# Undivided agent values in the product, a GpSimd fold of the sums, and a linear product issued in steps: agent attention with a maxout layer

## The chip, the cores and the metric

The kernel runs on one core of a Trainium2 chip. The metric is the device time of one execution in microseconds (us). Six runs of the kernel before gave a median of 465.62 us, from 465.35 to 466.1. The profile comes from one execution, so times inside it are compared with that execution's own time. PE is TensorE, PEld its weight loads, DVE is VectorE, ACT is ScalarE, POOL is GpSimd, and SP is SyncE, which issues the transfers.

## The reference, cut to what matters

```
a2k     = softmax(scale * agents @ k^T)      # per batch: 49 agents over 12544 keys
agent_v = a2k @ v                            # 49 x 128
q2a     = softmax(scale * q @ agents^T)      # 12544 queries over 49 agents
x       = q2a @ agent_v                      # 4 batches: 50176 rows of 128
h       = max(x @ w1, x @ w2, x @ w3)        # 768 wide
out     = h @ w_out
```

There are 4 batches. The softmax of the agents over the keys divides each agent's row of `agent_v` by one number, the sum of that agent's exponentials.

## The kernel before, in words

**What is computed.** The maxout is rewritten with differences: max(x w1, x w2, x w3) = x w1 + max(0, x (w2 - w1), x (w3 - w1)) (one of the six slices uses w3 - w2 in place of w3 - w1). So each batch needs a small matrix G: agent_v times the weights' differences (columns C31 and C21, 768 each) and agent_v times w1 w_out (256 columns from C1O, the linear part, for two row halves). A query group then needs only its exponentials `e_q`, G and `w_out`. The 128 partitions are split in two halves (h) of 64, each with the 49 agents, for even and odd rows.

**Key groups.** Keys are worked in groups of up to nine 128-row tiles (`k_group`): load k and v (SP), cast to bf16 (POOL for k; ACT or POOL for v), transpose k, scores (L291, PE), exponentials (L296, ACT), values (L302, PE), and an addition into `Vacc` (L312, DVE). The first batch's twelve groups run before any query ("early"). They transpose on PE (L273) and copy the result on DVE (L279), and they sum the exponentials with a matmul against ones (L305, 49 columns, giving every partition the sum of each agent, in `Vacc`'s columns 49 to 97). The later three batches' groups are hosted one by one in query groups, share their small PSUM tile, and add their exponentials on POOL into `Eacc` (L319). Two of these transpose on PE, the rest by a DMA issued from SP (L275).

**The tail of a batch's keys** (`k_tail`). `reduce` sums `Eacc` over its nine positions on DVE (L363, 441 to 49 columns). `total` sums it over the partitions with a float32 matmul against ones (L368). `normalise` takes the reciprocal (L374), clears 15 columns (L376) and multiplies `Vacc` by it into `avT` (L377). `product` multiplies `avT` by pieces of the weights (L389), and DVE (L394) or ACT (L396) copies the result into G.

**Query groups** (`q_group`, 49 of them, s = 0 to 48, each 8 tiles): cast, transpose (L454 and the copy L459, or a DMA), scores (L474), exponentials (L480), their sums (L488) and reciprocals (L494). Then for six slices f: `first` (u, L500), `relu_first` (a, L515, or L512 in place for one slice), `second` (v, L500) and `max_second` (x, L525 on DVE, or L523 on ACT). Then the output: `out_linear` (L530, needs G's linear part), `out_hidden` (L539) and `out_scale` (L546), and the store (L553).

**The order.** Every step is put on a list with a key by `at`, and `emit` issues them sorted by key, one program order for all engines; a query group spans 6.0 keys, and the tables KEY, LATE, BORDER and BEGIN give each step's place in it. A step whose needs are not met, or whose ring of buffers is not free, is held back until they are. The rings are "uv" (3 PSUM tiles of two banks for u, v and products), "om" (2 small PSUM tiles, for query transposes, scores, the hosted key work and outputs) and "a". Each engine then runs its own instructions in this order and waits on semaphores.

**Borders and the ramp.** Query groups 12, 24 and 36 are the first that need the next batch's G; the group before each runs the tail of its keys (the "border"). The "ramp" is the change from the early groups to the steady order, groups 0 and 1. There `ramp` issues six filler matmuls (L624) of 512 columns in place of the output matmuls of a group that does not exist. `prep_linear1` computes w1 w_out (six matmuls, L227, and a copy on ACT, L228), and the third piece of G's product follows it. `keep_busy` (L233) issues other fillers.

Of the kernel before, what the change touches and what calls it, by code (L numbers as in the profile page):

```python
# [9 lines left out]
FP32 = mybir.dt.float32  # L10
BF16 = mybir.dt.bfloat16
# [5 lines left out]
def kernel(  # L17
# [18 lines left out]
    nc = tc.nc  # L36
# [130 lines left out]
    agT = const.tile([P, B, H], BF16, name="agT")  # L167
    nc.vector.memset(agT, 0.0)
    sel = const.tile([P, 2], BF16, name="sel")
    nc.vector.memset(sel, 0.0)  # L170
# [52 lines left out]

    def prep_linear1():
        t = small_tile("o_ps")
        for f in range(NF):
            nc.tensor.matmul(t[:, :C], w1T[:, f, :], wo_bf[:, f, :], start=(f == 0), stop=(f == NF - 1))  # L227
        nc.scalar.activation(wall[:, C1O + C:C1O + 2 * C], t[:, :C], AF.Copy)  # L228

# [13 lines left out]
    def k_group(b, t0, n, key, s):  # L243
# [38 lines left out]
        def scores():  # L282
            if early:
                d["pair"] = uv_tile()
                d["s"] = d["pair"][:, 0, :]
                last_tile["t"] = d["s"]
            else:
                d["s"] = host[s]
            t = d["s"]
            for j in range(n):  # L290
                nc.tensor.matmul(t[:, j * A:(j + 1) * A], d["kT"][:, j, :], agT[:, b, :A],  # L291
                                 start=(j == 0), stop=True, skip_group_check=True)

        def exps():
            d["e"] = work.tile([P, KT * A], BF16, tag="e_k", bufs=3, name="e_k")
            nc.scalar.activation(d["e"][:, :n * A], d["s"][:, :n * A], AF.Exp, scale=scale)  # L296

        def values():
            t, c = (d["pair"][:, 1, :], 0) if early else (d["s"], CV)
            for j in range(n):  # L300
                e = d["e"][:, j * A:(j + 1) * A]
                nc.tensor.matmul(t[:, c:c + A], d["vb"][:, j, :], e, start=(early and j == 0),  # L302
                                 stop=True, skip_group_check=True)
                if early:
                    nc.tensor.matmul(t[:, A:2 * A], ones_bf, e, start=False, stop=True,  # L305
                                     skip_group_check=True)

        def add_values():
            w = 2 * A if early else A
            src = d["pair"][:, 1, :w] if early else d["s"][:, CV:CV + A]  # L310
            if t0:
                nc.vector.tensor_tensor(out=Vacc[b], in0=src, in1=Vacc[b], op=ALU.add)  # L312
            else:
                Vacc[b] = work.tile([P, w], FP32, tag=f"Vacc{w}", name="Vacc")
                nc.vector.tensor_copy(out=Vacc[b], in_=src)
# [42 lines left out]
    def k_tail(b, sum_key, keys, s):  # L358
        d = {}

        def reduce():
            d["e"] = work.tile([P, A], FP32, tag="e_sum", name="e_sum")
            nc.vector.tensor_reduce(out=d["e"], in_=Eacc[b].rearrange("p (j a) -> p a j", a=A),  # L363
                                    axis=mybir.AxisListType.X, op=ALU.add)

        def total():
            d["s"] = host[s]
            nc.tensor.matmul(host[s][:, :A], ones, d["e"], start=True, stop=True,  # L368
                             skip_group_check=True)

        def normalise():

            r = (last_tile["t"] if s is None else d["s"])[:, :A]
            nc.vector.reciprocal(r, Vacc[b][:, A:] if s is None else r)  # L374
            d["avT"] = work.tile([P, H], BF16, tag="avT", name="avT")
            nc.vector.memset(d["avT"][:, A:], 0.0)  # L376
            nc.vector.tensor_tensor(out=d["avT"][:, :A], in0=Vacc[b][:, :A], in1=r, op=ALU.mult)  # L377
            G[b] = work.tile([P, WC], BF16, tag="G", name="G")

        def product(c0, c1, on_vector):  # L380
            t = uv_tile()
            cuts = [c for c in range(c0, c1, 512)] + [c1]
            for i, (a, z) in enumerate(zip(cuts, cuts[1:])):
                for lo, hi in ((a, min(z, C1O)), (max(a, C1O), z)):
                    for h in range(2 if lo < hi else 0):


                        c = lo + (C if lo >= C1O and h == 0 else 0)
                        nc.tensor.matmul(t[h * H:(h + 1) * H, i, lo - a:hi - a], d["avT"],  # L389
                                         wall[:, c:c + hi - lo], start=True, stop=True,  # L390
                                         skip_group_check=True)
            src = t.rearrange("p i c -> p (i c)")[:, :c1 - c0]
            if on_vector:
                nc.vector.tensor_copy(out=G[b][:, c0:c1], in_=src)  # L394
            else:
                nc.scalar.activation(G[b][:, c0:c1], src, AF.Copy)  # L396

        if s is not None:
            at(sum_key - 1, reduce, ("sum_e", b), [("kx", s - 1)])
            at(sum_key, total, ("total", s), [("sum_e", b), ("ho", s)])  # L400
        at(sum_key + (0.9 if s is None else 0.01), normalise, ("normalise", b),
           [("ka", ("early", NT - last_size)) if s is None else ("total", s)])

        pieces = ((C31, C1O), (C21, C31), (C1O, WC)) if s is None else ((C31, WC), (C21, C31))
        for i, (c0, c1) in enumerate(pieces):
            on_vector = s is None and i == 0
            at(keys[i], lambda c0=c0, c1=c1, on_vector=on_vector: product(c0, c1, on_vector),
               ("product", b, i), [("normalise", b)] + ["lin_b"] * (i == 2), "uv", [("product", b, i)])

# [12 lines left out]
    def q_group(s):  # L422
# [132 lines left out]
        new = [("product", tails[s], i) for i in range(2)] if s in tails else []  # L555
        new_linear = new if s else [("product", 0, 2)]

# [54 lines left out]
    def ramp():  # L612

        for o in range(1, 2):
            at(KEY[f"lin{o}"] - 6, lambda: d_fill.update(t=small_tile("o_ps")), ("fill", o), (), "om",
               [("filled", o)])
            keys = sorted(KEY[f"oc{o}{f}"] for f in range(NF))
            for i, key in enumerate(keys):
                at(key - 6, fill, ("filled", o) if i == NF - 1 else None, [("fill", o)])

    d_fill = {}

    def fill():
        nc.tensor.matmul(d_fill["t"], ident, busy, start=True, stop=True, skip_group_check=True)  # L624

# [4 lines left out]
    first_key = last_key - 6.0 * (len(first_sizes) - 1)  # L630
    last_size = first_sizes[-1]
    at(first_key - 35, prep, "prep", (), "om", ["prep"])
    at(first_key - 6.5, load_weights)
# [3 lines left out]
    at(last_key - 3.24, prep_w_out)  # L637
    at(4.5, prep_linear1, "lin_b", ["lin_a"], "om", ["lin_b"])
    fillers = []
    for g, n in enumerate(first_sizes):  # L640
        k_group(0, sum(first_sizes[:g]), n, first_key + 6.0 * g, None)

        if 4 <= g < len(first_sizes) - 5:
            fillers += [(first_key + 6.0 * g + 0.55, 3), (first_key + 6.0 * g + 1.3, 3)]
    k_tail(0, last_key, (last_key + 0.95, last_key + 1.02, 4.8), None)
    for key, n in fillers + [(last_key + 0.9, 2), (last_key + 1.1, 2),
# [47 lines left out]
```

## Time and profile before

| what | value |
|---|---|
| median of six runs | 465.62 us |
| the profiled execution: its time / its span | 466.1 us / 464.3 us |
| granted TensorE clock | 1.000 |
| PE busy | 437.1 us (94%), 5450 matmuls |
| DVE busy | 405.7 us (87%) |
| ACT busy | 396.4 us (85%) |
| POOL busy | 167.1 us (36%) |
| L525, maximum on DVE | 245 of 1220 ns |
| L539, output matmuls on PE | 2352 |
| L363, reduction on DVE | 3 of 946 ns |
| L319, additions on POOL (441 columns) | 27 of 1026 ns |

Busy time of an engine is a share of the whole span, and the stages have different limits, so the stages are read apart. A matmul's length in the rows is about 0.2 to 0.4 us with its way through the array, and the next starts long before it ends: what matmuls cost is read from start to start. In the time line, a bracket after a row gives the idle time before it and what ended it.

### The profile page before, as it was taken

The page shows a single profiled execution, that of the slowest core. Times are in us where ns is not written, and L with a number is a line of the kernel's source. Part 1 is how long each engine was busy: PE and PEld are TensorE (multiplying, and loading weights), DVE is VectorE, ACT ScalarE, POOL GpSimd, SP SyncE. Part 2 cuts the span into 40 slices and gives each one's busy share as a digit, 9 for nine tenths or more (in the row PEclk, how much of TensorE's full clock was granted, in tenths as well). Part 3 has the DMA queues.
Part 4 walks back from the last instruction along what each step waited for, and adds up shares of the span by engine and source line. Part 5 has one row for each costly group of instructions (what it writes and reads, how often), then busy time and mean ns, then how long its engine had stood idle before and what let it go on. Part 6 is the DMA issues. An engine that isn't in the chain of part 4 may idle for free.

```text
span 464.3 us, 13292 instructions
## 1 busy us (share of the span) xinstructions
PE 437.1 (94%) x5450; PEld 274.7 (59%) x5450; DVE 405.7 (87%) x516; ACT 396.4 (85%) x461; POOL 167.1 (36%) x167
## 2 busy tenths in 40 slices
PE   2497899999999999999999999999999999999996
PEld 2375466666665766666656666666656555555554
DVE  3165699999998999999999999999998999999995
ACT  3356889989899999899889898998999999999992
POOL 2244963553450544536262446354230010100000
PEclk9999999999999999999999999999999999999999
DMA  8999999999998999998997999996846668553222
GB/s 317 409 410 392 409 284 380 292 350 213 310 288 285 288 287 324 317 271 221 293 335 246 288 315 306 293 257 182 186 114 180 162 172 171 163 134 114 69 85 98
DMA packets 82632, 118.53 MB, mean 255 GB/s; under 512 B 56391, under 2 KB 57867, under 8 KB 82571
## 3 DMA queue, kind: packets, MB, share of 16 engines
q1 hardware_dynamic: 82368, 117.59, 84.3%
q8 instruction: 42, 0.69, 0.6%
q14 instruction: 19, 0.16, 0.1%
q10 hardware_dynamic: 203, 0.10, 0.1%
HBM read 78.74 MB, written 25.69 MB: 225 GB/s over the span
## 4 chain that ended last, share of the span: by engine, by line
PE 82%; DMA 6%; ACT 6%; issue 2%; DVE 2%; POOL 0%; SPq 0%; ACTq 0%; POOLq 0%; DVEq 0%
PE uv_ps L500 34%; PE o_ps L539 28%; PE o_ps L530 5%; DMA st<-in_k_dram 4%; PE m_ps L454 4%; ACT a_sb L515 3%; PE m_ps L474 3%; DVE r L525 2%; DMA st<-in_v_dram 2%; PE m_ps L291 1%; PE m_ps L302 1%; PE m_ps L233 1%; PE m_ps L488 1%; ACT uv_ps L512 1%; PE uv_ps L273 1%
## 5 line engine op out<-in xcount | busy, mean ns | idle before, releaser
L525 DVE TENSOR_TENSOR r<-uv_ps,a_sb 128x1024 bf16<-128x1024 f32 x245 | 297.3, 1220 | 16.0 <-PE uv_ps L500 5.3
L515 ACT ACTIVATE a_sb<-uv_ps 128x1024 bf16<-128x1024 f32 x245 | 240.8, 1027 | 13.7 <-PE uv_ps L500 12.2
L500 PE MATMUL uv_ps<-e_q,G 49*128 49x512 bf16 (+3 forms) x1248 | 186.6, 368 | 2.2 <-ACT a_sb L515 0.6
L539 PE MATMUL o_ps<-wo_bf,r 128*128 128x128 bf16 x2352 | 174.8, 220 | 0.2 <-DVE r L525 0.2
L539 PEld LDWEIGHTS <-r 128*128 128x128 bf16 x2352 | 137.8, 98 | 39.8 <-issue 37.8
L500 PEld LDWEIGHTS <-G 49*128 49x128 bf16 x1248 | 58.1, 93 | 63.8 <-issue 31.8
L319 POOL TENSOR_TENSOR Eacc<-Eacc,e_k 128x441 f32<-128x441 f32 (+1 forms) x30 | 30.5, 1016 | 129.4 <-ACT e_k L296 129.4
L546 DVE TENSOR_TENSOR o_sb<-o_ps,recips 128x512 f32<-128x512 f32 x98 | 67.5, 689 | 9.7 <-PE o_ps L539 7.0
L449 POOL CAST q_bf<-st 128x1024 bf16<-128x1024 f32 x49 | 51.0, 1042 | 62.9 <-DMA qT<-q_bf 61.5
L523 ACT ACTIVATE r<-uv_ps 128x1024 bf16<-128x1024 f32 x49 | 50.2, 1024 | 20.3 <-PE uv_ps L500 20.1
L259 POOL CAST k_bf<-st 128x1152 bf16<-128x1152 f32 (+2 forms) x45 | 50.6, 1125 | 27.9 <-DMA st<-in_k_dram 21.3
L512 ACT ACTIVATE uv_ps<-uv_ps 128x1024 f32<-128x1024 f32 x49 | 49.5, 1011 | 0.9 <-ACT a_sb L515 0.4
L530 PE MATMUL o_ps<-G,e_q 128*128 128x256 bf16 x196 | 38.1, 276 | 0.0
L266 POOL CAST v_bf<-st 128x1152 bf16<-128x1152 f32 (+1 forms) x33 | 37.5, 1136 | 0.6 <-ACT e_q L480 0.3
L480 ACT ACTIVATE e_q<-m_ps 128x512 bf16<-128x512 f32 x49 | 29.8, 608 | 0.5 <-PE m_ps L474 0.5
L279 DVE COPY kT<-uv_ps 128x1152 bf16<-128x1152 bf16 (+1 forms) x14 | 9.9, 710 | 17.5 <-PE uv_ps L273 17.5
L264 ACT ACTIVATE v_bf<-st 128x1152 bf16<-128x1152 f32 (+1 forms) x12 | 12.9, 1071 | 14.1 <-DMA st<-in_v_dram 14.1
L530 PEld LDWEIGHTS <-e_q 128*128 128x128 bf16 x196 | 12.4, 97 | 18.9 <-issue 18.2
L454 PEld LDWEIGHTS <-q_bf 128*128 128x128 bf16 x264 | 14.9, 98 | 12.8 <-issue 10.4
L273 PE MATMUL uv_ps<-ident,k_bf 128*128 128x128 bf16 x116 | 11.6, 262 | 11.0 <-POOL k_bf L259 10.4
L459 DVE COPY qT<-m_ps 128x1024 bf16<-128x1024 bf16 x32 | 21.8, 680 | 0.2 <-PE m_ps L454 0.2
L454 PE MATMUL m_ps<-ident,q_bf 128*128 128x128 bf16 x264 | 20.4, 220 | 0.3 <-POOL q_bf L449 0.3
(68 smaller groups left out, 233.7 us busy)
## 6 DMA issues: line engine op xcount, KB each, us to landing
st<-in_q_dram SPq DMA_DIRECT2D x46, 512.0 KB, 4.7
out_dram<-o_sb SPq DMA_DIRECT2D x46, 512.0 KB, 3.5
st<-in_k_dram SPq DMA_DIRECT2D x40, 576.0 KB, 6.9
st<-in_v_dram SPq DMA_DIRECT2D x40, 576.0 KB, 7.8
st<-in_k_dram SPq DMA_DIRECT2D x3, 512.0 KB, 6.5
st<-in_v_dram SPq DMA_DIRECT2D x3, 512.0 KB, 6.5
wst<-in_moe_w_dram SPq DMA_DIRECT2D x3, 384.0 KB, 10.5
st<-in_q_dram SPq DMA_DIRECT2D x2, 384.0 KB, 4.7
```

Of the source, the lines that this page charges most:

```text
L259: nc.gpsimd.tensor_copy(out=d["kb"][:, :n, :], in_=d["k"][:, :n, :])
L266: nc.gpsimd.tensor_copy(out=d["vb"][:, :n, :], in_=d["v"][:, :n, :])
L449: nc.gpsimd.tensor_copy(out=d["qb"], in_=d["q"])
L454: nc.tensor.transpose(t[:, j * P:(j + 1) * P], d["qb"][:, j, :], ident)
L500: nc.tensor.matmul(t[:, h, j0 * P:j1 * P], G[b][h * H:h * H + A, col + f * P:col + (f + 1) * P], d["e"][h * H:h * H + A, j0 * P:j1 * P], s ...
L512: nc.scalar.activation(u, u, AF.Relu)
L515: nc.scalar.activation(a_sb[f], u, AF.Relu)
L523: nc.scalar.activation(r, v_ps[f], AF.Relu)
L525: nc.vector.tensor_tensor(out=r, in0=v_ps[f], in1=a_sb[f], op=ALU.max)
L530: nc.tensor.matmul(t[:, i * 2 * C:(i + 1) * 2 * C], d["e"][:, jj * P:(jj + 1) * P], G[batch[jj]][:, C1O:C1O + 2 * C], start=(i == 0), stop ...
L539: nc.tensor.matmul(t[:, c:c + C], r_sb[f][:, h, jj * P:(jj + 1) * P], wo_bf[:, f, :], start=False, stop=True, skip_group_check=True)
L546: nc.vector.tensor_tensor(out=d["out"][:, j:j + m, :], in0=d["o", o].rearrange("p (j c) -> p j c", c=C), in1=d["r"][:, j:j + m].unsqueeze( ...
```

## The change

Six things change, and nothing else in the order's keys.

1. `avT`, the agent values, is written undivided, in bf16, by the addition of the batch's last key group. It is one fixed tile for all batches, cleared at the start. The product uses it as it is. The division moves to the copies of the product into G: each is scaled per partition (per agent) by `r_ag`, on DVE with `tensor_scalar_mul`, on ACT with a scale read from SBUF.
2. `r_ag` is the reciprocal of one column per batch (128x1 in place of 128x49). For this, the sum of the exponentials must lie along the partitions: in `total`, the sums become the stationary operand, and a column of ones streams, once for each half.
3. In the early groups the matmul against ones goes. Each tile's exponentials are loaded as the stationary operand (64 columns, the last 15 set to one beforehand) twice, once for each half, against one column of ones. The exponentials lie in three fixed tiles with rows of 64. `Vacc` is 50 columns wide in place of 98. The last group adds its column into PSUM, where the reciprocal reads it.
4. `reduce` moves from DVE to POOL: four additions in SBUF (196, 98, 49 and 49 columns), placed right after the batch's last `add_exps`.
5. The six filler matmuls of the ramp go. The six matmuls of w1 w_out are issued one by one in their places, into a small tile that is taken where the fillers' tile was.
6. The third piece of the first G's product leaves its "uv" tile: it is written into other columns of that small tile, after the copy on ACT (now behind group 1's a0), and copied out scaled behind group 1's a1. The small tile is held until then.

```diff
+    avT = const.tile([P, B, H], BF16, name="avT")
+    nc.vector.memset(avT, 0.0)
+    e_sum = const.tile([P, H], FP32, name="e_sum")
+    nc.vector.memset(e_sum[:, A:], 1.0)
+    r_ag = const.tile([P, B], FP32, name="r_ag")
+    e_first = [const.tile([P, KT, H], BF16, name=f"e_first{i}") for i in range(3)]
+    for t in e_first:
+        nc.vector.memset(t[:, :, A:], 1.0)
...
+    def prep_linear1(f):
+        nc.tensor.matmul(linear["t"][:, :C], w1T[:, f, :], wo_bf[:, f, :], start=(f == 0),
+                         stop=(f == NF - 1))
+
+    def linear_out():
+        nc.scalar.activation(wall[:, C1O + C:C1O + 2 * C], linear["t"][:, :C], AF.Copy)
+
+    def linear_product():
+        for h in range(2):
+            c = C1O + (1 - h) * C
+            nc.tensor.matmul(linear["t"][h * H:(h + 1) * H, C:3 * C], avT[:, 0, :], wall[:, c:c + 2 * C],
+                             start=False, stop=True, skip_group_check=True)
+
+    def linear_product_out():
+        nc.scalar.activation(G[0][:, C1O:WC], linear["t"][:, C:3 * C], AF.Copy, scale=r_ag[:, 0:1])
...
-                if early:
-                    nc.tensor.matmul(t[:, A:2 * A], ones_bf, e, start=False, stop=True,
-                                     skip_group_check=True)
+            for j in range(n if early else 0):
+                for h in range(2):
+                    nc.tensor.matmul(t[h * H:(h + 1) * H, A:A + 1], d["e"][:, j, :], ones_bf[:, :1],
+                                     start=False, stop=True, skip_group_check=True)
...
+            if t0 + n == NT:
+                nc.vector.tensor_tensor(out=avT[:, b, :A], in0=src[:, :A], in1=Vacc[b][:, :A], op=ALU.add)
                 if early:
+                    nc.vector.tensor_tensor(out=src[:, A:], in0=src[:, A:], in1=Vacc[b][:, A:],
+                                            op=ALU.add)
...
         def reduce():
-            d["e"] = work.tile([P, A], FP32, tag="e_sum", name="e_sum")
-            nc.vector.tensor_reduce(out=d["e"], in_=Eacc[b].rearrange("p (j a) -> p a j", a=A),
-                                    axis=mybir.AxisListType.X, op=ALU.add)
+            w = KT // 2 * A
+            t = Eacc[b]
+            while w >= A:
+                nc.gpsimd.tensor_tensor(out=t[:, :w], in0=t[:, :w], in1=t[:, w:2 * w], op=ALU.add)
+                w = w // A // 2 * A
+            nc.gpsimd.tensor_tensor(out=e_sum[:, :A], in0=t[:, :A], in1=t[:, KT * A - A:], op=ALU.add)
 
         def total():
-            d["s"] = host[s]
-            nc.tensor.matmul(host[s][:, :A], ones, d["e"], start=True, stop=True,
-                             skip_group_check=True)
+            for h in range(2):
+                nc.tensor.matmul(host[s][h * H:(h + 1) * H, :1], e_sum, ones[:, :1], start=True,
+                                 stop=True, skip_group_check=True)
 
         def normalise():
-
-            r = (last_tile["t"] if s is None else d["s"])[:, :A]
-            nc.vector.reciprocal(r, Vacc[b][:, A:] if s is None else r)
-            d["avT"] = work.tile([P, H], BF16, tag="avT", name="avT")
-            nc.vector.memset(d["avT"][:, A:], 0.0)
-            nc.vector.tensor_tensor(out=d["avT"][:, :A], in0=Vacc[b][:, :A], in1=r, op=ALU.mult)
+            src = last_tile["v"][:, A:A + 1] if s is None else host[s][:, :1]
+            nc.vector.reciprocal(r_ag[:, b:b + 1], src)
             G[b] = work.tile([P, WC], BF16, tag="G", name="G")
...
             if on_vector:
-                nc.vector.tensor_copy(out=G[b][:, c0:c1], in_=src)
-            else:
-                nc.scalar.activation(G[b][:, c0:c1], src, AF.Copy)
+                nc.vector.tensor_scalar_mul(G[b][:, c0:c1], src, r_ag[:, b:b + 1])
+            else:
+                nc.scalar.activation(G[b][:, c0:c1], src, AF.Copy, scale=r_ag[:, b:b + 1])
...
-            at(sum_key - 1, reduce, ("sum_e", b), [("kx", s - 1)])
+            at(6.0 * (s - 1) + table(s - 1)["ke"] + 1.51, reduce, ("sum_e", b), [("kx", s - 1)])
...
-        for o in range(1, 2):
-            at(KEY[f"lin{o}"] - 6, lambda: d_fill.update(t=small_tile("o_ps")), ("fill", o), (), "om",
-               [("filled", o)])
-            keys = sorted(KEY[f"oc{o}{f}"] for f in range(NF))
-            for i, key in enumerate(keys):
-                at(key - 6, fill, ("filled", o) if i == NF - 1 else None, [("fill", o)])
+        at(KEY["lin1"] - 6, linear_tile, "linear", ["lin_a"], "om", ["lin_c"])
+        keys = sorted(KEY[f"oc1{f}"] for f in range(NF))
+        for f, key in enumerate(keys):
+            at(key - 6, lambda f=f: prep_linear1(f), ("linear", f), ["linear"])
+        key = 6 + KEY["a0"] + 0.01
+        at(key, linear_out, "linear_out", [("linear", f) for f in range(NF)])
+        at(key + 0.4, linear_product, "lin_b", ["linear_out"])
+        at(6 + KEY["a1"] + 0.01, linear_product_out, "lin_c", ["lin_b", ("normalise", 0)])
```

## The prediction

> **What bounds the kernel now.** I read the stage table first (busy time of each engine in chosen windows), because the shares over the whole span mix a load-bound start with a TensorE-bound body. Its columns are the window, its length, then PE, PEld, DVE, ACT and POOL busy with instruction counts, the granted clock, the DMA share and GB/s.
>
> ```profile
> 2.00:46.00 44.00, 27.88 (x451) 21.99 (x451) 18.23 (x41) 21.74 (x29) 15.73 (x15) 1.00 1.02 398
> 46.00:62.00 16.00, 14.15 (x155) 7.55 (x155) 11.52 (x16) 13.12 (x17) 14.78 (x15) 1.00 1.06 364
> 62.00:124.00 62.00, 61.73 (x793) 39.05 (x790) 59.09 (x73) 56.64 (x68) 28.01 (x27) 1.00 1.08 314
> 124.00:149.00 25.00, 24.49 (x289) 15.04 (x288) 23.57 (x32) 22.36 (x27) 10.37 (x10) 1.00 0.95 276
> ```
>
> Up to 46 us the DMA engines run at 398 GB/s while every engine has gaps: transfers set the pace. From 62 us PE has 61.73 of 62 us, DVE 59.09, ACT 56.64: PE sets it, the others close behind. In that steady body the 20-matmul piece of L539 recurs in the chain every 8.35 us. The clock is 1.00 everywhere. The fourth row is a border between two batches. There the same piece is 34.95 us apart over four groups (127.83 to 162.78) instead of 4 x 8.35 = 33.40, so a border costs 1.55 us, and the three together cannot repay more than 4.7.
>
> Second, the chain of work that ended last, in the ramp, where group 1 starts:
>
> ```profile
> 54.12 0.43 PE o_ps L624 x2
> 54.56 0.82 PE uv_ps L500 x6
> 55.38 0.77 PE o_ps L624 x3
> 56.15 0.04 issue
> 56.19 0.51 PE o_ps L227 x6
> 56.70 0.02 issue
> 56.72 0.29 ACT wall L228
> 57.01 0.04 issue
> 57.05 0.30 PE uv_ps L389 x2
> ```
>
> Six filler matmuls (L624; these five and one at 53.58), then the six of the linear product (L227), ScalarE's copy of it (L228), then its product with the agent values (L389). All of it is on the path, one behind the other.
>
> Third, the first border in the time line, VectorE and then PE (start, length, what, idle before it and its releaser):
>
> ```profile
> 134.40 0.95 DVE L363 TENSOR_REDUCE e_sum<-Eacc 128x49 f32<-128x441 f32 x1
> ...
> 136.52 0.48 DVE L374 RECIPROCAL m_ps<-m_ps 128x49 f32<-128x49 f32 x1
> ```
>
> ```profile
> 136.06 0.42 PE L368 MATMUL m_ps<-e_sum,ones 128*128 128x49 f32 x2 [0.43 <-ACT e_q L480]
> ```
>
> The total (L368) comes after 0.43 us of idle that an exponential on ScalarE ends, not the reduction on VectorE, which was over at 135.35. Fourth, the DMA issues: one transfer, group 2's transposed keys, issued by SP at 53.43; its last column is the time to landing, so it lands at 62.83.
>
> ```profile
> kT<-k_bf SPq DMA_TRANSPOSE x1, 9.4
> ```
>
> **The ramp.** The six fillers (about 0.22 each: three in a row start to end take 0.82, of which 0.38 is one matmul's length) go, 1.3 us. L227's six, in their places, are about 0.055 apart (0.49 less one 0.22, over five), 0.33 in all. The block at 56.19 to 57.3 goes. I follow the new order with the old durations. u0 and u1 of group 1 still wait for ScalarE (54.4) and for a VectorE maximum (near 55.0), so u1 ends at 55.25. Three L227 end at 55.4, the values and sums (0.33) at 55.75. ScalarE: a0 54.95 to 55.9 (it was 55.14), the linear copy to 56.15. The linear product then runs to 56.45: PE waits 0.4 for that copy, but the next matmuls (v0) need x5, which VectorE ends only at 56.2, so the added wait costs about 0.25. v0 and u3 end at 56.87 (58.02 and later before). The linear tile keeps one of the two small PSUM buffers until ScalarE has copied it out (a1 to 57.05, copy 0.38 as the old 128x256 row, 57.4), so group 2's query transposes, and lin0 and v1 queued behind them, stand until 57.45. They end at 58.0, as against 58.57; lin0, oc, v1 at 58.67. v3 now finds u3 rectified at 58.35 (it was 60.07, since u3 had waited for the extra PSUM tile), and the 20-matmul piece starts near 59.1 instead of 60.66. PE is 1.5 us early.
>
> That is not all kept. Group 2's key scores stand at 64.07; 1.5 earlier is 62.55, and their operand lands at 62.83. That transfer was issued at 53.43, before any gain, behind loads at 100% DMA share, so it does not move. With 0.1 for the release (0.05 from a cast's end at 45.18 to its matmul), PE passes at 62.93: gain **1.15**. Later transposes have room: issue 60.36 plus 9.1 is 69.5, needed at 72.4. POOL waits only for ScalarE there (34.5 us in 62 to 132), so nothing upstream takes it back, and a PE-bound body carries it to the end.
>
> **The early groups** pay and gain under cover. Each position's 49-column sum (L305, about 0.025 behind its neighbour) becomes two one-column matmuls, each with a load of 64 columns. No row has that shape: the 2-column L488 is 0.02 to 0.025 apart, the 64-column loads of L474 0.034 apart, and one whole such load lasts 0.107 (L389). I take 0.034, the row with the same load: 18 x 0.034 - 9 x 0.025 = 0.39 a group. Followed through the last groups, with PE's waits of 0.85, 0.26 and 0.24 taking part of it, the last values end at 42.5 instead of 41.84. VectorE then saves: 0.47 + 0.07 + 0.21 (reciprocal, memset, product) leave the way to the product, and avT comes out of the last addition. The product starts at 43.0 (43.32 before). Neither matters: u0 stands behind the transposes of the keys cast at 44.02 to 45.17, which waited for a landing at 43.94. Cover: about 1.1 us for the first G piece. The exponentials keep their elements, so nothing is counted for their new rows. The added memsets (some 1 us) lie in VectorE's 3.48 us wait for the agents. The two small operations for r_ag (0.2 each by the 128x8 reciprocal, 197 ns) run beside the product.
>
> **The borders.** Removed from VectorE: 0.95 + 0.48 + 0.07 + 0.21; added 0.2. VectorE is idle for want of others soon after (0.44 at 140.7, for ScalarE's G; 0.22 for PE), so I count nothing for it, bound 0 to 0.5 a border. POOL adds four additions of 196, 98, 49 and 49 columns: by L319 (1026 ns for 441, 931 for 392; 1.94 ns a column and 0.17) 0.55 + 0.36 + 2 x 0.27 = 1.45 us, from 133.44 to 134.9, 1.1 ahead of the total. The casts queued behind move 1.45 later; they feed work two groups on, and at the third border POOL then idles 4.36 anyway. The total becomes four loads and matmuls of 64 columns; two of 128 occupied PE for 0.35. By the column this is the same; bounds -0.15 and +0.8 (four at 0.19 + 0.11 with no overlap). I take 0.
> A rule speaks against the fold: the Trainium skill's "GPSIMD Engine Reference", section "When to use GPSIMD", has a free-axis reduction belong to VectorE. The rows agree on the price (1.45 against 0.95), which would count only if POOL were on the path.
>
> The evacuations of G get a per-row scale. No row of ScalarE has one. Copies of 128x1024 and 128x768 take 1042 and 831 ns, so 0.2 is fixed; the scale adds between nothing and one more fixed part, I take 0.1. Only the second piece is in the chain (0.71 at 149.71, and at 251.50; not at the third border): +0.2 in all, bounds 0 and 0.6 if all six count at 0.1.
> The Trainium skill's "ScalarE: Activation LUTs", section "What ACT_TABLE_LOAD costs", gives about 93 ns for each pointer operand; no row here shows it. By it these two would cost 0.19, and all six 0.56.
>
> **Sum.** The profiled execution took 466.1 (span 464.3 and 1.8 around it). -1.15 + 0.2 = -0.95 gives 465.15. The median of the runs is 465.62, 0.48 below that execution, and the same step gives **464.7**. Own range: 464.1 (fixed by the landing, plus the VectorE bound of 0.5 once) to 465.2 (all six scales and a little of the total). A measurement tells about 0.2% from no change, 0.93 us, so this stands just at that bound.
>
> **Rivals.**
> *The gain is larger* (0.20): the transposes land earlier or only part of them is waited for, so 1.5 stays, and VectorE's freed 1.5 us lets PSUM buffers go sooner at each border, up to 0.5 each. For it: VectorE has no idle from 124 to 140 in a border, and groups of four L500 take 0.64 to 0.74 there instead of 0.54 to 0.6. Against: the waits named are for ScalarE and PE. 465.62 - 1.5 - 1.0 = 463.1.
> *The gain is lost in the new waits* (0.17): the buffer held by the linear tile stops PE longer than 0.6, or the landing comes later with the fuller queue; 0.3 to 0.5 remains, against 0.2 to 0.6 for the scales. 465.6.
> *Slower* (0.15): the early sums. 106 small matmuls take the place of 53 within 34 to 42 us, where PE idles 2.07. At a price p the addition is 106p - 1.3: 2.3 at 0.034 (covered), 5.0 at 0.06, when u0 is delayed about 1.2 and the ramp's gain is gone. From about 0.07 the kernel is slower; at 0.107, no load overlapped, 10 us are added, 2 covered by idle, and with loads still landing meanwhile some 3 reach the end after the gain: 468. For it: 64-column loads one by one do last 0.107. Against: the pace of 0.034. Halfway, 466.8.
> The likeliest (0.48) is the sum. That the change does not do what it says is excluded as far as the code goes: the fillers and the late block are gone from the order.
>
> **Numbers.** Of the likeliest's 0.48, half lies beyond 0.2%: faster 0.24 + 0.20 and a little of the next = 0.46; within 0.2%: 0.24 + 0.15 = 0.39; slower 0.15. Range 463.2 to 466.5: it leaves out the lower half of the larger gain and most of the slower case.
>
> **To look for.** The 20-matmul piece near 59.2 in the ramp, and a PE wait of some 0.3 for kT at 62.5 to 62.9; if PE does not wait there and is 1.5 early, the larger gain is right. Early sums' pace (0.034). POOL's fold ending before the total. G's evacuations 0.1 longer. Borders still 34.9 to 35.1 over four groups. Wrong if the early groups' last values end after 43, if PE waits on the linear tile past 57.5, or if borders move by over 0.3.

## The result, and the profile after

The changed kernel takes 467.05 us (median of 20 runs, 465.62 to 469.07); the kernel before took 465.69 us beside it (40 runs). The ratio is 1.0028, with an interval from 1.002 to 1.0036: slower, by 1.3 us, where 464.7 had been forecast, and just above the range. The profiled execution took 467.65 us and its span is 465.9 us, 1.55 longer than before's.

The same four stages as in the prediction, now of the kernel after (window, length, busy time of PE, PEld, DVE, ACT and POOL with their instructions, granted clock, DMA share, GB/s):

```profile
2.00:46.00 44.00, 30.10 (x534) 24.46 (x536) 16.74 (x42) 20.74 (x27) 16.02 (x15) 0.92 1.02 397
46.00:62.00 16.00, 14.40 (x150) 7.31 (x147) 11.84 (x16) 13.37 (x18) 14.46 (x15) 0.91 1.09 377
62.00:124.00 62.00, 61.96 (x804) 39.26 (x801) 59.03 (x74) 56.94 (x68) 28.02 (x28) 1.00 1.02 302
124.00:149.00 25.00, 24.29 (x294) 14.92 (x292) 22.40 (x29) 22.49 (x27) 11.89 (x14) 1.00 0.90 294
```

The loads run as they did (397 GB/s), the body as well. What is new stands in the column behind POOL: the granted clock is 0.92 and 0.91 in the two early stages, where before's table prints 1.00. The page of the kernel after has it in its row of clocks, a digit for each 11.65 us:

```profile
PEclk9996899999999999999999999999999999999999
```

In finer windows of the same trace the place is plain:

```profile
38.00:40.00 2.00, 1.89 (x54) 1.73 (x49) 0.78 (x3) 1.83 (x4) 0.85 (x2) 0.67 1.08 353
40.00:42.00 2.00, 1.88 (x39) 1.71 (x39) 0.84 (x3) 0.34 (x2) 1.04 (x1) 0.50 1.06 391
42.00:44.00 2.00, 1.79 (x31) 1.64 (x31) 0.59 (x3) 0.38 (x2) 0.32 (x1) 0.50 1.04 411
44.00:46.00 2.00, 2.00 (x12) 0.88 (x12) 0.17 (x1) 1.02 (x1) 1.73 (x2) 0.50 1.00 401
46.00:48.00 2.00, 2.00 (x18) 1.16 (x15) 1.02 (x1) 1.46 (x2) 1.98 (x3) 0.50 1.03 410
48.00:50.00 2.00, 1.78 (x10) 0.42 (x9) 0.76 (x1) 0.66 (x2) 1.96 (x3) 0.77 1.02 409
```

The trace's own clock records put half clock from 38.69 to 48.93 us: 10.24 us, three times 3.41. This is the end of the early groups and the preparation of the first query group. What half clock does is seen in rows of the same shape. PE's time line before (start, length):

```profile
42.30 0.62 PE L454 MATMUL m_ps<-ident,q_bf 128*128 128x128 bf16 x8 [0.30 <-POOL q_bf L449]
...
45.23 0.68 PE L273 MATMUL uv_ps<-ident,k_bf 128*128 128x128 bf16 x9 [0.47 <-POOL k_bf L259]
...
46.27 0.88 PE L500 MATMUL uv_ps<-e_q,G 49*128 49x512 bf16 x6
```

and after:

```profile
37.73 0.45 PE L336 MATMUL uv_ps<-ones_bf,e_first 128*64 128x1 bf16 x18
...
43.36 1.03 PE L489 MATMUL m_ps<-ident,q_bf 128*128 128x128 bf16 x8
...
47.03 1.14 PE L297 MATMUL uv_ps<-ident,k_bf 128*128 128x128 bf16 x9
...
48.96 0.82 PE L535 MATMUL uv_ps<-e_q,G 49*128 49x512 bf16 x6
```

The query's transposes take 1.03 instead of 0.62, the keys' 1.14 instead of 0.68. Before, PE waited for casts (the brackets); after, the casts are done by then and from 42.5 us to the first slice PE waits for nobody. Group 0's first slice (L500, now L535) starts at 48.96 instead of 46.27: 2.69 us late.

Half clock is not new in these kernels. The clock's records begin with its first rise, at 28.43 us in before and 25.03 in after, and the windows and pages count the time ahead of it as full. PE's rows of before show the pace there:

```profile
22.86 1.14 PE L273 MATMUL uv_ps<-ident,k_bf 128*128 128x128 bf16 x9 [5.12 <-POOL k_bf L259]
...
30.49 0.66 PE L273 MATMUL uv_ps<-ident,k_bf 128*128 128x128 bf16 x9
```

So the 1.00 that before's table prints for 2 to 46 us holds from 28.43 on alone; ahead of that nine transposes took 1.14 in before too. What the change adds is a second stretch of half clock, later, that lasts up to group 0's first slice.

From the first slice on the ramp is faster, as forecast. Rows of PE after:

```profile
56.20 0.23 PE L239 MATMUL o_ps<-wo_bf,w1T 128*128 128x128 bf16 x1
...
58.95 0.30 PE L248 MATMUL o_ps<-wall,avT 128*64 128x256 bf16 x2 [0.29 <-ACT wall L243]
...
61.69 1.29 PE L574 MATMUL o_ps<-wo_bf,r 128*128 128x128 bf16 x20
```

The six matmuls of w1 w_out lie among the others, PE's wait for their copy is 0.29, and the 20-matmul piece starts at 61.69, 1.03 later than before's 60.66. So 2.69 - 1.03 = 1.66 us is gained between the first slice and this piece.

In the chain of the kernel after, what is left of before's block is the copy on ACT, behind a0, and the product; the fillers are gone:

```profile
58.73 0.18 ACT wall L243
58.91 0.04 issue
58.95 0.30 PE o_ps L248 x2
```

The first border in the time lines of POOL and PE:

```profile
134.24 1.39 POOL L401 TENSOR_TENSOR Eacc<-Eacc 128x196 f32<-128x196 f32 x3
135.71 0.29 POOL L403 TENSOR_TENSOR e_sum<-Eacc 128x49 f32<-128x49 f32 x1
```

```profile
136.87 0.28 PE L407 MATMUL m_ps<-ones,e_sum 128*64 128x1 f32 x4 [0.52 <-ACT e_q L515]
```

The fold ends at 136.00 and the total still starts behind an exponential on ScalarE, as before. The 20-matmul pieces around this border start at 128.55 and 163.61: 35.06 apart, 0.11 more than before. Group 2's transposed keys (issue at 53.07, the last column is the time to landing) land at 62.47, and nobody waits:

```profile
kT<-k_bf SPq DMA_TRANSPOSE x1, 9.4
```

Added up by the ends of groups, the 1.55 us are: +2.69 of half clock, -1.66 of the linear product, +0.26 at the three borders, and +0.26 of single stalls in the body (net: one of 0.30 is gone, 0.20 and 0.35 are new), of which more below.

### The profile page after: what moved, and what is told of

Same layout as the page of the kernel before. It is cut to its first block, busy times and chain, and to the rows that moved or that the text cites. A ratio compares the mean times of both kernels' runs of the same rounds, so it can differ in the third digit from the quotient of the medians.

```text
span 465.9 us, 13503 instructions
## 1 busy us (share of the span) xinstructions
PE 440.1 (94%) x5548; PEld 276.9 (59%) x5548; DVE 401.1 (86%) x511; ACT 397.3 (85%) x461; POOL 171.6 (37%) x179
## 4 chain that ended last, share of the span: by engine, by line
PE 79%; DMA 7%; ACT 7%; DVE 4%; issue 2%; SPq 1%; POOL 0%; ACTq 0%; POOLq 0%; DVEq 0%
PE uv_ps L535 33%; PE o_ps L574 27%; PE o_ps L565 5%; DMA st<-in_k_dram 5%; ACT a_sb L550 5%; PE m_ps L489 4%; DVE r L560 3%; PE m_ps L509 3%; DMA st<-in_v_dram 2%; PE m_ps L315 1%; PE m_ps L332 1%; PE m_ps L523 1%; ACT uv_ps L547 1%; PE uv_ps L424 1%; ACT e_q L515 1%
## 5 line engine op out<-in xcount | busy, mean ns | idle before, releaser
L535 PE MATMUL uv_ps<-e_q,G 49*128 49x512 bf16 (+3 forms) x1248 | 186.7, 368 | 2.6 <-ACT a_sb L550 0.7
L535 PEld LDWEIGHTS <-G 49*128 49x128 bf16 x1248 | 57.2, 93 | 64.4 <-issue 32.7
```

Source lines behind the costliest of these rows:

```text
L535: nc.tensor.matmul(t[:, h, j0 * P:j1 * P], G[b][h * H:h * H + A, col + f * P:col + (f + 1) * P], d["e"][h * H:h * H + A, j0 * P:j1 * P], s ...
```

## The experiments

Theory C: the one-column early sums take streamed columns away from TensorE, its clock is halved over the end of the early groups and does not come back until group 0 is in full work, and that is what makes it slower. The rivals of the expectations: P, the early sums' price by the piece (the prediction's own rival); B, the borders; L, the linear product's new waits; others are named where they first occur. The runs were made in three sets, each beside the kernel before: its median was 465.91 us beside runs 1 to 4, 465.89 beside 5 to 8 and 465.70 beside 9 to 12. A ratio is to the kernel before of its own set.

**1. The early sums as before, all else changed.**

```diff
-            for j in range(n if early else 0):
-                for h in range(2):
-                    nc.tensor.matmul(t[h * H:(h + 1) * H, A:A + 1], d["e"][:, j, :], ones_bf[:, :1],
-                                     start=False, stop=True, skip_group_check=True)
+                if early:
+                    nc.tensor.matmul(t[:, A:2 * A], ones_bf, e, start=False, stop=True,
+                                     skip_group_check=True)
```

(and the first batch divided as before.)

> The changed kernel with the early groups' sums as before (49 columns streamed against ones, batch 0 divided as before); all other parts stay. Theory C (the clock: the one-column sums lower PE's activity in the early groups, and the granted clock falls to 0.5 for one or more windows around 38 to 49 us, which makes the ramp late): the clock stays at 1.00 through the ramp, the ramp's gain of 1.1 to 1.6 us is kept, 464.3 to 465.0. Rival B (the loss lies at the borders and in the scaled copies): clock or not, 466 or more. Rival L (the new waits of the linear product in the ramp eat the gain): 465.6 to 466.2.

Measured: 465.93 us, ratio 1.0001 (0.999 to 1.0012). One half-clock window is left (36.67 to 40.08), and the first slice starts at 45.84. The loss is gone, so it comes with the early sums; the gain that C expected is not there. The next run says why.

**2. Only the linear product (parts 5 and 6) on the kernel before.**

```diff
-        for o in range(1, 2):
-            at(KEY[f"lin{o}"] - 6, lambda: d_fill.update(t=small_tile("o_ps")), ("fill", o), (), "om",
-               [("filled", o)])
...
+        at(KEY["lin1"] - 6, linear_tile, "linear", ["lin_a"], "om", ["lin_c"])
```

> The kernel before with the linear product in steps alone (parts 5 and 6). Theory C: group 1's first 20-matmul piece 1.1 to 1.6 us earlier, nothing else moved, clock 1.00: 464.1 to 464.6. Rival L: 465.5 to 466. Rival B says the same as C here.

Measured: 465.51 us, ratio 0.9994 (0.9981 to 1.0007). Its profiled execution is 1.07 shorter in span than before's, but before's profiled execution was a long one of its runs and this one a short one, so the medians, 0.40 apart, are what counts. PE's row for group 2's keys in this kernel:

```profile
62.87 0.40 PE L307 MATMUL m_ps<-agT,kT 128*128 128x49 bf16 x9 [0.96 <-DMA kT<-k_bf]
```

The prediction had put PE's pass at 62.93 with a wait of some 0.3 for this transfer. The pass is there; the wait is 0.96, since PE came earlier than forecast. C's 464.1 to 464.6 is missed, and the number lies at the edge of L's 465.5 to 466; but the wait that takes the gain is the one for group 2's keys, not one on the linear tile.

**3. Only the early sums (part 3, and the undivided values of the first batch) on the kernel before.**

```diff
-                if early:
-                    nc.tensor.matmul(t[:, A:2 * A], ones_bf, e, start=False, stop=True,
-                                     skip_group_check=True)
...
+                    nc.tensor.matmul(t[h * H:(h + 1) * H, A:A + 1], d["e"][:, j, :], ones_bf[:, :1],
+                                     start=False, stop=True, skip_group_check=True)
```

> The kernel before with the one-column early sums and the undivided agent values of batch 0 alone; later batches, fillers and linear product as before. Theory C: the clock falls to 0.5 in the ramp in most executions, 466.5 to 470, with a wide spread. Rival B: clock 1.00, 465.5 to 465.9. Rival L: 465.5 to 465.9.

Measured: 469.74 us, ratio 1.008 (1.0058 to 1.0102). Half clock from 36.37 to 50.02, four windows, and the first slice at 50.29, 4.02 later than before. The part by itself costs more than the whole change.

**4. The changed kernel with fillers beside more of the early groups.**

```diff
-        if 4 <= g < len(first_sizes) - 5:
+        if 4 <= g < len(first_sizes) - 2:
```

> The changed kernel with the fillers of the early groups (two times three 512-column matmuls a group) given to groups 4 to 9 in place of 4 to 6. Theory C: PE's activity is kept up and the clock stays at 1.00, 464.3 to 465.2. Rivals B and L: the fillers change nothing or cost a little, 466.5 to 467.5.

Measured: 466.23 us, ratio 1.0012 (1.0002 to 1.0022). The clock stays at 1.00 and more than half of the loss goes, as C has it; the time that C expected (464.3 to 465.2) is missed. The first slice starts at 47.54, not at 46.27: with the fillers (0.82 for each three) PE's rows cover all of 26.77 to 40.42 us, so the fillers themselves stand in PE's way.

**5. The changed kernel, its early sums over 49 columns of ones in place of one.** The same instructions, loads and order; only the streamed columns of 196 matmuls grow. The 48 added columns of each sum are not used.

```diff
-                    nc.tensor.matmul(t[h * H:(h + 1) * H, A:A + 1], d["e"][:, j, :], ones_bf[:, :1],
+                    nc.tensor.matmul(t[h * H:(h + 1) * H, A:2 * A], d["e"][:, j, :], ones_bf[:, :A],
```

> The changed kernel with the early sums' ones streamed as 49 columns in place of 1 (the first of them is read); same matmul count, same loads, same order, only the columns differ. Theory C in its sharper form (the clock follows the columns streamed per window of 3.41 us: in the profiles so far a window under about 3150 is followed by half clock, and half clock ends after a window over about 3600): at most one window at half clock around 35 to 40 us, u0 of group 0 near 46, 465.2 to 466.0. Rival P (the many small loads of 64 columns lengthen PE's path, the clock only goes with it): u0 at 48 or later, 467 or more, since PE has even more to do.

Measured: 465.71 us, ratio 0.9996 (0.9987 to 1.0005). More work for TensorE makes the kernel 1.3 us faster, and the loss is gone. Over its eleven runs the mean clock is 0.998 to 1.000, where the changed kernel's runs have 0.985 to 1.000. In this kernel's trace the clock stays full from its rise at 26.79 us on, and its page shows no fall:

```profile
PEclk9999999999999999999999999999999999999999
```

The first slice starts at 46.28 (before 46.27). A price of the matmul or of its load (P) can't do this, since neither got cheaper. That settles the loss. The gain of the ramp is still not there, and PE's next wait, for group 2's keys, shows where it goes:

```profile
63.51 0.40 PE L315 MATMUL m_ps<-agT,kT 128*128 128x49 bf16 x9 [0.92 <-DMA kT<-k_bf]
```

Here the transfer was issued at 53.44, as in before, and took 10.0 us to land.

**6. Only the borders (parts 1, 2 and 4 for the later three batches) on the kernel before.**

```diff
-            nc.vector.tensor_reduce(out=d["e"], in_=Eacc[b].rearrange("p (j a) -> p a j", a=A),
-                                    axis=mybir.AxisListType.X, op=ALU.add)
+            while w >= A:
+                nc.gpsimd.tensor_tensor(out=t[:, :w], in0=t[:, :w], in1=t[:, w:2 * w], op=ALU.add)
+                w = w // A // 2 * A
...
+                nc.scalar.activation(G[b][:, c0:c1], src, AF.Copy, scale=r_ag[:, b:b + 1])
```

> The kernel before with parts 1, 2 and 4 for batches 1 to 3 alone (undivided agent values, scaled copies on ScalarE, the fold on GpSimd, the new total); the early groups, batch 0 and the ramp as before. From the profiles' group times: +0.12, +0.12 and +0.04 at the three borders, 0.3 in all, and a single stall of 0.2 to 0.35 may move: 465.9 to 466.5. Theory B of the first set (the borders carry the loss) would say 467 or more.

Measured: 466.12 us, ratio 1.0007 (0.9999 to 1.0016): +0.2 (the interval reaches from 0.05 faster to 0.75 slower), where the prediction had +0.2. Theory B, that the borders are the loss, falls.

**7. The linear product of run 2, with the loads of one group issued behind group 2's key transposes.** If the landing at 62.87 clips the gain, what stands ahead of that transfer in the queue is to go behind it.

```diff
-            at(6.0 * s - 24.6, load)
+            at(3.01 if s == 4 else 6.0 * s - 24.6, load)
...
-            at(key - 26, load)
+            at(3.0 if s == 4 else key - 26, load)
```

> The kernel before with the linear product in steps, and the loads of group 4 (q, k, v) issued behind the transposes of group 2's keys in place of ahead of them. If the ramp's gain is cut by that landing (0.96 us of wait at the key scores of group 2 in the profile without this), the wait goes and the first 20-matmul piece of group 1 and everything behind is 0.7 to 1.0 earlier than there: 464.3 to 464.9. If the transposes wait for something else, or group 4's later loads come due, the same as without it or worse: 465.5 to 466.5.

Measured: 464.06 us, ratio 0.996 (0.9947 to 0.9972): faster than both kernels (median of five runs), and a little more than the 464.3 to 464.9 expected.

**8. The kernel before without fillers in its early groups.**

```diff
-        if 4 <= g < len(first_sizes) - 5:
+        if False:
```

> The kernel before without the fillers of early groups 4 to 6; the sums stay as they were, 49 columns. Theory C: some 2475 columns a group at one group in 2.96 us are 2850 a window, under the bound, so the clock is at 0.5 from the thirties to near 50 us in most executions: 467 to 471, without any of the changed kernel's parts. Rival P: PE has less to do and the small loads are absent: 465.4 to 466.

Measured: 465.80 us, ratio 1.0 (0.9991 to 1.0009). A miss. Full clock came at 30.05 us and stayed. The expectation had reasoned with the mean, 2475 columns for each early group every 2.96 us, that is 2850 in 3.41 us. The two windows that mattered held 3112 and 3627, since the groups do not lie evenly, and from 36.9 us the last early groups come closer together (their transposes start at 36.39, 37.98 and 39.31). So fillers are not what keeps the clock in before; run 12 asks the same of the changed kernel.

**9. The changed kernel with both repairs: 49 columns as in run 5 and the loads' order of run 7.**

> The changed kernel with its early sums over 49 columns and with the loads of group 4 behind group 2's key transposes: the two repairs together. With the sums over 49 columns alone the time was 465.71 and the group after the ramp ended 0.57 us ahead of before. Theory C (clock gate, then the landing of the keys): the order gives what it gave on the linear product alone, 1.75 - 1.21 = 0.54 us of the profile, so 0.5 to 1.4 us off the median: 464.3 to 465.3, with no half clock in the ramp; it stays above the 464.06 of the linear product and the order without the rest, by the borders' +0.2 to 0.3 and the single stalls' 0.2 to 0.6. Rival O (the order gains by itself, whatever the ramp does): the same 464.3 to 465.0, so this run doesn't tell it apart, the next one does. Rival S (what the other parts cost the rest of the run eats the gain): 465.6 or more.

Measured: 464.72 us, ratio 0.998 (0.9968 to 0.9992). PE's rows and the transfer in this kernel:

```profile
59.09 1.29 PE L574 MATMUL o_ps<-wo_bf,r 128*128 128x128 bf16 x20
...
62.51 0.39 PE L315 MATMUL m_ps<-agT,kT 128*128 128x49 bf16 x9
```

```profile
kT<-k_bf SPq DMA_TRANSPOSE x1, 5.3
```

The transfer lands 5.3 us after its issue instead of 10.0 as in run 5, PE's pass at 62.51 waits for nothing, and the 20-matmul piece starts at 59.09: the prediction had written "near 59.1". It stays 0.66 above run 7's kernel, which has neither the borders nor the early sums of the change.

**10. Only the loads' order, on the kernel before** (the edit of run 7 alone).

> The kernel before with nothing changed but the place of the loads of group 4, behind group 2's key transposes. Theory C: group 2's keys land earlier, but in before TensorE reaches their passes at 64.07 us, 1.2 us after the landing at 62.83, so nobody waits for them: 465.6 to 466.2, ratio within 0.9993 to 1.0007. Rival O (the order itself gains, through the queue or the evenness of the transfers, and the linear product adds only its 0.4): 464.3 to 465.2.

Measured: 465.69 us, ratio 0.9999 (0.999 to 1.0007). The order alone gives nothing, the linear product alone 0.4 (not clear of zero), the two together 1.83: where PE is not early, nobody waits for these keys.

**11. The changed kernel with the loads' order** (the edit of run 7 alone).

> The changed kernel as it is, with the loads of group 4 behind group 2's key transposes. Theory C: the half clock comes between 36 and 50 us, before this order can act, and makes u0 late by some 2.7 us; TensorE then reaches group 2's keys after their landing, so the order gains nothing: 466.6 to 467.6. Rival O: 465.3 to 466.2.

Measured: 467.12 us, ratio 1.0027 (1.0015 to 1.004), as the changed kernel. Half clock from 36.54 to 50.20, and the first slice at 50.38. The order can't repair what was lost ahead of it.

**12. The changed kernel without fillers in its early groups** (the edit of run 8).

> The changed kernel without the filling products of the early stage (nothing of its output depends on them). Its early groups then stream 2052 columns each, one every 2.96 us, 2364 in 3.41 us, and nothing else. Theory C: no window of the early stage reaches the 3500 to 3850 columns at which half clock was left, so the full clock comes only with the first full group; u0 is at 48.9 us or later, as in the changed kernel or up to 3 us worse: 466.8 to 470. The same edit of before, which streams 2475 columns a group, gave 465.80 and no half clock after 30 us, where 467 to 471 had been expected, since its first two windows at full clock held 3112 and 3627 columns. Rival N (the fillers and the columns don't decide; the fall of the clock was an accident of the order): 465.2 to 466.2, as that edit of before.

Measured: 467.48 us, ratio 1.0033 (1.0021 to 1.0045). PE's rows:

```profile
36.51 1.14 PE L297 MATMUL uv_ps<-ident,k_bf 128*128 128x128 bf16 x9 [0.28 <-POOL k_bf L283]
...
38.33 0.65 PE L336 MATMUL uv_ps<-ones_bf,e_first 128*64 128x1 bf16 x18
...
48.69 0.88 PE L535 MATMUL uv_ps<-e_q,G 49*128 49x512 bf16 x6
```

The transposes take 1.14 here too. The first record of the clock in this trace is its rise, at 47.31; the windows print 1.00 ahead of it, so ahead of the first record the rows' lengths are to be read instead. The same edit that cost before nothing (run 8) leaves this kernel at half clock from its start to just ahead of group 0's first slice.

**What the clock goes by.** In the early stage of all fourteen traces (before, after and the twelve runs) I added up from PE's matmul rows the columns that each streams (the last figure of its moving operand, 512 in 128x512), by windows of 3.41 us counted from the clock's first record; windows ahead of it are taken as half clock, as run 12's rows show them. A few per cent of the rows can be missing. Nine of the traces:

```
kernel                       columns in successive windows around the fall -> clock of the next
before                       6685, 4054, 4277, 6784                       stays full
after                        4104, 2858 | 1969, 3480, 5248 |              half for three windows
1 sums as before             6102, 2731 | 3858 |                          half for one
2 only linear                6053, 3115 | 3926 |                          half for one
3 only early sums            6164, 2168 | 2436, 2342, 2505, 6272 |        half for four
4 more fillers               5583, 6660, 3175, 8328                       stays full
5 sums over 49               6788, 3496, 5957, 5326                       stays full
8 before, no fillers         3112, 3627, 4895, 5953                       stays full
11 after, loads' order       5750, 2070 | 2564, 2263, 2968, 5248 |        half for four
```

The bars enclose the windows at half clock. Every window that was followed by half clock held 2070 to 3115 columns, every one that kept full clock 3112 or more. At half clock, every window with 3493 or more brought the full clock back and none under 2948; between these it went both ways. So kernels with the old early sums fall too, now and then (runs 1, 2, 6, 7 and 10 each show one window), but their next window streams enough to return. With one-column sums a group streams 1152 + 2 x 441 + 18 = 2052 columns instead of 1152 + 3 x 441 = 2475, and at half clock the following windows hold 1969 to 3480: the clock does not return until group 0's work streams more. PE's busy time does not tell the cases apart. Its rows cover 41 to 61% of the windows behind which the clock fell, and 54% or more of those behind which it stayed: 56% in after's window of 2858 columns and 56% in run 5's of 3496. This dependence is read off the traces and not varied finely; run 5 is the one that changes the columns and nothing else. Whether the chip itself counts columns, or something that goes with them, these runs do not show.

The changed kernel's runs go the same way by their mean clock (which counts the time ahead of the first record as full), not without scatter: 466.09 and 466.25 us at 0.999 and 1.000, 465.62 to 467.2 at 0.991 to 0.995, 467.28 to 468.06 at 0.987 and 0.988, 468.54 to 469.07 at 0.985.

## Why the prediction was wrong

**The step that failed** is "The early groups pay and gain under cover". It weighed the one-column sums as PE time against PE's idle (and its rival did so at other prices), with "The clock is 1.00 everywhere" taken from before as a given. That was a misreading already: before's own rows are at half pace up to 28.43 us. In these runs the clock is a result of the work: with 423 columns less per group, all that PE does from 38.69 to 48.93 goes at half pace. The tell-tale that the prediction named fired (wrong "if the early groups' last values end after 43": the last values end at 43.12, their sums at 43.43), and its cover of "about 1.1 us" was used up and 2.69 more. The rival on the slower side named the right part of the change with the wrong mechanism: it needed a price of 0.07 a matmul, and the sums are cheaper than assumed. That its 466.8 lies near the measured time is luck. At full clock eighteen last 0.45 with one matmul's own length of some 0.17 in it, so 0.0165 apart, not 0.034; at half clock eighteen last 0.64. The 0.034 came from one pair of loads of L474 (0.14 for the two, at 134.32); another pair in before took 0.11 (at 62.41), which is one load's own length.

The Trainium skill's "TensorE: Matmul & The Clock Gate", section "Part 1: The HAM clock gate", says that a monitor watches TensorE in free-running windows of 3413 ns and halves its clock when it has been idle. The width is that of these traces (10.24 us is three). Under "HAM oscillation — how this bites in real kernels" the page asks for no PE-idle gap over 3.4 us. By that the changed kernel would have kept its clock: its longest gap around the window of the fall was 1.59 us, and PE's rows covered 56% of that window and 94% of the next, which stayed at half. In these traces it is the streamed columns of a window that go with the fall.

**The ramp** was right in its mechanism and in its 1.5: from the first slice to the 20-matmul piece 1.66 is gained in the changed kernel, 1.67 in run 9, 1.74 in run 7. **The clip** was right in its place (62.87 in run 2 against 62.93) and too small in what it took: the transfer landed 9.5 us after its issue in run 2 and 10.0 in run 5, so the passes stood at 62.87 and 63.51, and over the runs the linear product alone gave 0.40 us instead of 1.15 (its interval reaches from 0.9 faster to 0.3 slower). One part of the difference lies in the step from the profile to the median, which the prediction took to be the same. Before's profiled execution was 0.48 us above its median. In run 10, whose ramp is before's and whose profiled execution took 465.59, this pass stands at 63.43 and waits for nobody, 0.64 earlier than the 64.07 of before's profile; its first slice is as much earlier (45.62 against 46.27). From there to run 2's 62.87 is 0.56 and not 1.20, so an execution near the median has less to gain up to the landing. That is an estimate from two traces; that it and the landing's scatter are the whole of the difference was not shown. That the landing is the clip was shown, by runs 7 and 10. So even with the clock kept the forecast of 464.7 would have been missed: run 5 has 465.71, within 0.2% of before.

**The borders** came as written: +0.26 by the ends of groups, +0.2 by run 6 (not clear of zero), against 0.2. The evacuations of G, by shape, after and then before (lines, shapes, count, busy, mean ns, idle):

```profile
L431 ACT ACTIVATE G<-uv_ps,r_ag 128x768 bf16<-128x768 f32 x4 | 3.7, 918 | 0.1
L431 ACT ACTIVATE G<-uv_ps,r_ag 128x1024 bf16<-128x1024 f32 x3 | 3.4, 1128 | 0.0
```

```profile
L396 ACT ACTIVATE G<-uv_ps 128x768 bf16<-128x768 f32 x4 | 3.3, 831 | 0.1
L396 ACT ACTIVATE G<-uv_ps 128x1024 bf16<-128x1024 f32 x3 | 3.1, 1042 | 0.0
```

87 and 86 ns more, against the 0.1 taken. The Trainium skill's "ScalarE: Activation LUTs", section "What ACT_TABLE_LOAD costs", has 93 for a pointer operand, which these rows bear out. The fold takes 1.76 us on POOL (1.45 forecast) and ends before the exponential that the total waits for, as forecast; VectorE's freed 1.5 us a border bought nothing that the ends of groups show.

## What to carry to other kernels

Where TensorE idles part of the time and its clock is full, count the columns that a change takes out of each window of 3.41 us before calling its work covered: making small matmuls smaller can halve TensorE's clock, and with it the pace of all its other work in that stretch. Read the clock from rows of the same shape too, since the records say nothing ahead of their first one. Before a gain is written down, look at what its followers wait for next and when that was issued: here one reordered load was worth 1.0 to 1.4 us (run 9 against 5, run 7 against 2), but only together with the gain, and nothing alone. A single profiled execution can be 0.7 us off the median difference of two kernels, so a step of that size is checked on the runs.

## What was not expected of the hardware

- A window's streamed columns, not its busy time, went with the fall of the clock: 3112 columns at 55% busy kept it (run 8), 2858 at 56% (after) and 2070 at 58% (run 11) lost it.
- A transpose by DMA landed 9.4 to 11.0 us after its issue behind the loads of another group (ten traces), and 5.3 with these behind it (four); SP's own issue of it fell from 5.2 to 1.35 us.
- Single stalls of 0.2 to 0.4 us in the steady body sit at places that go with the kernel: before and runs 2, 7 and 8 have one of 0.3 near 108 us; the changed kernel and run 5 have 0.2 near 177 and 0.35 near 372, and run 6 0.37 near 380. Net they are +0.26 of the changed kernel's 1.55. Nothing was tried on them, and their cause stays open.
